# A dynamic convolution and a gated feed-forward on one core: a re-ordered ramp, and x tiles loaded whole

## The chip, the cores and the metric

The kernel runs on one core of a Trainium2 chip. The metric is the device time of one execution in microseconds (us); quoted times are medians of the runs of one kernel. The core has the engines PE (matmul; its weight loads are listed apart as PEld), DVE (VectorE), ACT (ScalarE), POOL (GpSimd) and SP (SyncE, which here only issues DMA), and 16 DMA engines.

A profile is of one execution. Its span is some 1.9 us shorter than the time of the same execution (before: span 767.6, time 769.51), so spans are compared with spans only.

## The reference, cut to what matters

```python
# x: (8, 4096, 192), weight_gen: (8, 4096, 8 heads, 7 taps)
w = softmax(weight_gen, axis=-1)
x_pad = concatenate([zeros((8, 6, 192)), x], axis=1)       # causal: 6 rows of zeros first
out[b, s, h, g] = sum over k of w[b, s, h, k] * x_pad[b, s + k, h, g]
# then, on all 32,768 tokens
h = out @ w_in             # 192 -> 2048
g = h - tanh(h)
return g @ w_out           # 2048 -> 192
```

## The kernel before

The tokens are taken in 32 blocks of 1,024. A partition holds 8 consecutive tokens and the 6 rows ahead of them (the halo). Four blocks make one sequence of 4,096, so blocks 0, 4, 8, ..., 28 start a sequence, and partition 0 of those needs zeros for a halo.

For a block, POOL scales the softmax weights (wsm) and makes seven tap products of 2.9 us, into the tiles even, odd and last. One accumulating DMA then adds the odd taps to the even ones. PE sums what is left by matmuls with an identity (tile pc); this stretch has small matmuls close together, and I call it the conv stretch. ACT evicts it as convT. (Blocks 0 to 2 go without the accumulating DMA: PE sums all their taps.) PE then does the first matmul into ph, ACT a tanh, DVE the subtraction into gt, and PE the second matmul into an output bank (obank), one block behind.

```python
xpool = ctx.enter_context(tc.tile_pool(name="xpool", bufs=2))
...
def load_x(n):
    ...
    if n == 0:
        rows(0, P, HALO, HALO + J); rows(16, P, 0, HALO); rows(1, 16, 0, HALO)
        no_halo()                      # copies a row of zeros into the halo of partition 0
    elif s == 0:                       # start of a sequence
        no_halo()
        rows(0, 1, HALO, HALO + J)
        rows(1, 16)
        rows(16, P)
    else:
        rows(0, P)                     # the whole tile, 1,344 KB
...
for n in range(NTOT):
    if n + 3 < NTOT:
        load_wg(n + 3)
        load_x(n + 3)
    for p in range(J):
        gemm1(n, 2 * p); gemm1(n, 2 * p + 1)
        ...
        if p == 0 and 1 <= n < NTOT - 2:
            products(n + 2, behind=last_sub[0] if n > 1 else None)
        if 1 <= n < NTOT - 1 and p == 6:
            ...                        # conv stretch of block n + 1
```

xpool has two buffers, so the load of block n + 2 is issued when POOL ends its last tap of block n: POOL's pace sets the moment of every x load. And the argument `behind` holds POOL's scale until PE and DVE have come far enough, so that POOL can't run away from them.

The softmax here doesn't subtract the row's maximum and nothing guards it: scores larger than these inputs give would overflow.

## Time and profile before

| | before |
|---|---|
| time, median of 3 runs | 768.26 us (768.07 to 768.48) |
| the profiled run | 769.51 us, span 767.6 us |
| POOL, one block | 22.64 us, without a pause in it |
| PE, one block, undisturbed | 22.56 us |
| chain of what ended last | PE 93% |

The prediction below shows the views that it rests on. Beside them, the page gives these: first the busy time of each engine (share of the span, number of instructions), then two groups of instructions (line, engine, operation, tiles, shapes and count; busy time and mean ns of one; idle time before them and what ended it).

```profile
PE 737.2 (96%) x14784; PEld 577.8 (75%) x14784; DVE 652.8 (85%) x595; ACT 637.1 (83%) x865; POOL 695.3 (91%) x290
...
L197 POOL TENSOR_TENSOR odd<-x_t,wsm 128x1536 bf16<-128x1536 f32 x93 | 270.0, 2904 | 0.0
...
L206 POOL DMA_DIRECT2D even<-odd x29 | 34.9, 1205 | 9.1 <-POOL odd L197 9.1
```

POOL's 91% hides that it is full: its work ends near 713 us, and 695.3 us of it are done by then. So PE and POOL are bound together, and what matters is how far PE runs behind POOL. I measure that as a **distance**: from POOL's issue of the accumulating DMA of a block to PE's first conv matmul of that block. A large distance means that PE has fallen behind. It can't be much under 8.8 us, since the DMA itself lands 8.8 us (median) after its issue.

PE's waits after the ramp (40 to 760 us; what PE waited for, us in total, times, longest) are short. Most of their time is "issue", that is, a wait for nothing that the profile names; these are its two longest lines:

```profile
PE pc L240 <- issue: 4.5, 6, 3.2
PE obank L306 <- issue: 0.6, 1, 0.6
```

PE's instructions come in pages by DMA (queue q8 of the profile, "instruction", moved 1.88 MB in 115 packets, 16 KB each).

### The profile page before, as it was taken

The numbers are of one execution on the slowest core, as the hardware profiler recorded it, in microseconds if no ns is written. First come the engines' busy times: TensorE is split into PE (matmuls) and PEld (weight loads), VectorE is DVE, ScalarE is ACT, GpSimd is POOL, SyncE is SP. The second block draws the span as 40 slices with busy tenths as digits, with TensorE's granted clock in tenths as the row PEclk, the third lists the DMA queues.
The fourth block names the chain that finished last, engine by engine and source line by source line (L and its number), as shares of the span: only waits on it lengthen the run. The fifth ranks groups of instructions, "written<-read, shape, count | busy, mean of one in ns | idle before, by whom it ended". The sixth has DMA issues, their size and how long they took to land.

```text
span 767.6 us, 32329 instructions
## 1 busy us (share of the span) xinstructions
PE 737.2 (96%) x14784; PEld 577.8 (75%) x14784; DVE 652.8 (85%) x595; ACT 637.1 (83%) x865; POOL 695.3 (91%) x290
## 2 busy tenths in 40 slices
PE   2798999999999999999999999999999999999997
PEld 2276787777777777777777777777778777777777
DVE  7886898888888888889888889888888988888883
ACT  1876888888888888888888888888888888888883
POOL 6999999999999999999999999999999999999100
PEclk9999999999999999999999999999999999999999
DMA  7913776555677555577655567755556765542412
GB/s 216 202 56 87 182 181 161 119 138 150 164 182 176 135 129 145 149 178 183 166 125 129 150 160 182 180 126 139 144 149 175 182 174 114 129 141 77 98 44 84
DMA packets 25989, 111.37 MB, mean 145 GB/s; under 512 B 4815, under 2 KB 9855, under 8 KB 21893
## 3 DMA queue, kind: packets, MB, share of 16 engines
q1 hardware_dynamic: 14830, 77.00, 30.2%
q0 software_dynamic: 10816, 31.99, 25.8%
q8 instruction: 115, 1.88, 1.0%
q10 hardware_dynamic: 208, 0.34, 0.2%
q14 instruction: 20, 0.16, 0.1%
HBM read 54.49 MB, written 25.17 MB: 104 GB/s over the span
## 4 chain that ended last, share of the span: by engine, by line
PE 93%; DVE 3%; POOL 1%; issue 1%; DMA 1%; ACT 0%; SPq 0%; POOLq 0%
PE obank L306 43%; PE ph L273 43%; PE pc L240 6%; DVE gt L285 2%; PE po L341 1%; DMA x_t<-zero 1%; POOL even L197 1%; ACT th L284 0%; POOL odd L197 0%; SPq L107 0%; DVE zr L156 0%; DVE zsum L150 0%; ACT convT L254 0%; SPq L93 0%; DVE out_sb L353 0%
## 5 line engine op out<-in xcount | busy, mean ns | idle before, releaser
L285 DVE TENSOR_TENSOR gt<-ph,th 128x1024 bf16<-128x1024 f32 x512 | 602.7, 1220 | 94.6 <-ACT th L284 92.1
L284 ACT ACTIVATE th<-ph 128x1024 f32<-128x1024 f32 x512 | 497.4, 1022 | 65.9 <-PE ph L273 65.2
L306 PE MATMUL obank<-w_out,gt 64*128 64x192 bf16 x7936 | 399.2, 243 | 1.4 <-issue 0.6
L306 PEld LDWEIGHTS <-gt 64*128 64x128 bf16 x7936 | 351.4, 94 | 52.6 <-issue 1.2
L273 PE MATMUL ph<-convT,w_in 64*128 64x512 bf16 x3072 | 384.8, 378 | 6.3 <-DVE gt L285 5.1
L197 POOL TENSOR_TENSOR even<-x_t,wsm 128x1536 bf16<-128x1536 f32 x94 | 273.0, 2904 | 3.1 <-DMA x_t<-zero 0.7
L197 POOL TENSOR_TENSOR odd<-x_t,wsm 128x1536 bf16<-128x1536 f32 x93 | 270.0, 2904 | 0.0
L273 PEld LDWEIGHTS <-w_in 64*128 64x128 bf16 x3072 | 176.4, 94 | 112.1 <-issue 18.8
L325 ACT ACTIVATE out_sb<-obank 128x192 f32<-128x192 f32 x248 | 82.4, 332 | 30.6 <-PE obank L306 23.5
L197 POOL TENSOR_TENSOR last<-x_t,wsm 128x1536 bf16<-128x1536 f32 x31 | 103.4, 3335 | 0.0
L240 PE MATMUL pc<-ident,even 64*128 64x64 bf16 x2304 | 70.3, 191 | 3.7 <-POOL even L197 2.4
L240 PEld LDWEIGHTS <-even 64*128 64x128 bf16 x2304 | 64.7, 96 | 5.0 <-POOL even L197 2.7
L254 ACT ACTIVATE convT<-pc 128x1024 bf16<-128x1024 f32 x64 | 48.8, 808 | 14.9 <-PE pc L240 14.8
L206 POOL DMA_DIRECT2D even<-odd x29 | 34.9, 1205 | 9.1 <-POOL odd L197 9.1
L168 POOL TENSOR_TENSOR wsm<-e_t,zr 128x448 f32<-128x448 f32 x30 | 41.7, 1391 | 0.0
L240 PE MATMUL pc<-ident,last 64*128 64x64 bf16 x768 | 23.2, 192 | 8.5 <-DVE last L197 8.3
L140 ACT ACTIVATE e_t<-wg_t 128x448 f32<-128x448 f32 x32 | 18.5, 577 | 7.0 <-DMA wg_t<-in_weight_gen_dram 7.0
L240 PEld LDWEIGHTS <-last 64*128 64x128 bf16 x768 | 17.0, 96 | 8.7 <-DVE last L197 8.3
L240 PE MATMUL pc<-ident,odd 64*128 64x64 bf16 x448 | 16.2, 199 | 6.7 <-issue 3.9
L150 DVE TENSOR_REDUCE zsum<-e_t 128x64 f32<-128x448 f32 x32 | 19.5, 609 | 3.0 <-ACT e_t L140 3.0
L156 DVE RECIPROCAL zr<-zsum 128x64 f32<-128x64 f32 x30 | 16.6, 554 | 3.0
L240 PEld LDWEIGHTS <-odd 64*128 64x128 bf16 x448 | 11.8, 100 | 7.4 <-issue 4.2
(20 smaller groups left out, 48.7 us busy)
## 6 DMA issues: line engine op xcount, KB each, us to landing
x_t<-in_x_dram SPq DMA_DIRECT2D x24, 1344.0 KB
even<-odd POOLq DMA_DIRECT2D x29, 1024.0 KB, 8.8
out_dram<-out_sb SPq DMA_DIRECT2D x31, 768.0 KB
x_t<-in_x_dram SPq DMA_DIRECT2D x7, 1176.0 KB
wg_t<-in_weight_gen_dram SPq DMA_DIRECT2D x32, 224.0 KB
x_t<-in_x_dram SPq DMA_DIRECT2D x7, 157.5 KB
x_t<-in_x_dram SPq DMA_DIRECT2D x1, 768.0 KB
w_out<-in_moe_w_out_dram POOLq DMA_DIRECT2D x1, 768.0 KB, 9.1
```

What stands on the lines that cost most here:

```text
L140: nc.scalar.activation(out=e_t[:].rearrange("p j h k -> p (j h k)"), in_=wg_t[:].rearrange("p j h k -> p (j h k)"), func=ACT.Exp,)
L150: nc.vector.reduce_sum(out=zsum[:], in_=e_t[:].rearrange("p j h k -> p (j h) k"), axis=AX.X)
L168: return eng.tensor_mul(wsm.rearrange("p j h k -> p (j h) k"), e_t[:].rearrange("p j h k -> p (j h) k"), zr.rearrange("p (n o) -> p n o", ...
L197: eng.tensor_mul(dst[k].rearrange("p c j h g -> p j h c g"), x_t[:, k : k + J, :].rearrange("p j (h c g) -> p j h c g", h=H, c=NC), w[:, : ...
L206: nc.gpsimd.dma_start(out=even[:].rearrange("p i c j h g -> p (i c j h g)")[:, 0:ACC], in_=odd[:].rearrange("p i c j h g -> p (i c j h g)" ...
L240: nc.tensor.matmul(pc[:, r, col : col + R], lhsT=prods[c][gi][r * R : (r + 1) * R, c, 2 * j : 2 * j + 2].rearrange("p j h g -> p (j h g)") ...
L254: nc.scalar.activation(out=conv_of[n][:, c0 : c0 + nch, :].rearrange("p c (j r t) -> p r (c j) t", r=2, t=R), in_=pc[:, :, 0 : nch * JH * ...
L273: nc.tensor.matmul(ph[:, r, :], lhsT=w_in[r * R : (r + 1) * R, c, f * P : (f + 1) * P], rhs=convT[r * R : (r + 1) * R, c, :], start=(c == ...
L284: last_act[0] = nc.scalar.activation(out=th[:], in_=ph_f, func=ACT.Tanh)
L285: last_sub[0] = nc.vector.tensor_sub(gt[:], ph_f, th[:])
L306: mm = nc.tensor.matmul(po[:, 0:D], lhsT=g_of[n][f][r * R : (r + 1) * R, col : col + P], rhs=w_out[r * R : (r + 1) * R, f, :], start=(r == ...
L325: last_act[0] = nc.scalar.activation(out=out_sb[:, j, :], in_=po[:, 0:D], func=ACT.Copy)
```

## The change

The intent: let POOL start its first tap before the halo has come, let PE begin block 1 earlier, and simplify the x loads at the starts of sequences. In words: the taps of block 0 are split by tokens, so that pieces that need no halo run first, between DVE and POOL; the loads of w_in start with the first exponential; ACT copies the first seven tiles of w_in to the upper partitions where a DMA did; x of block 1 waits for a product of block 0; the conv sums of block 1 are made in the idle output banks; block 1's weights are scaled on POOL; and every x tile but the first is one load, with the zero copy after it.

```diff
-        elif s == 0:
-            no_halo()
-            rows(0, 1, HALO, HALO + J)
-            rows(1, 16)
-            rows(16, P)
         else:
-            rows(0, P)
+            dma = rows(0, P)
+            if behind is not None:
+                order(dma, behind, "order of the loads")
+            if s == 0:
+
+                no_halo()
...
+    load_w_in(0, FA, last_exp[0])
     softmax_norm(0, obank[0])
...
     products(
         0,
-        on_vector=(6, 3, 4, 5),
-        order_of=(6, 0, 3, 1, 4, 5, 2),
-        sums=(6, 3, 0, 4, 5, 1, 2),
-        hooks={2: rest_of_w_in},
+        taps=[
+            (G_, 6, 0, J),     # engine, tap, first and last token of a partition
+            (V, 5, 1, J),
+            (V, 4, 2, J),
+            (V, 5, 0, 1),
+            (V, 4, 0, 2),
+            (G_, 0, 0, J),
+            (V, 3, 0, J),
+            (V, 2, 0, J),
+            (G_, 1, 0, J),
+        ],
+        sums=(6, 5, 4, 3, 0, 2, 1),
+        hooks={1: rest_of_w_in},
     )
+    load_x(1, first_halo[0])
...
+    for c in range(NC):
+        nc.scalar.activation(out=w_in[R:P, c, 0:FA], in_=w_in[0:R, c, 0:FA], func=ACT.Copy)
...
+                if p == 3:
+                    pcs = []
+                    sums = conv_sums(1, ((0, 1),), pcs, obank)
```

(The comment on the tuple is mine; the moves of the softmax of blocks 2 and 3 and some helpers are cut.)

More of the change, by code (lines that the diff above doesn't have):

```diff
@@ L78 @@
     last_sub = {}
-    last_wsm = {}
+    last_exp = {}
+    first_halo = {}
     def order(inst, other, reason):
@@ L97, in load_wg, with load_x @@
         wg_of[n] = wg_t
-    def load_x(n):
+    def load_x(n, behind=None):
         b, s = divmod(n, NSB)
@@ L105, in rows @@
         def rows(p0, p1, r0=0, r1=HALO + J):
-            win = x[b, s0 + p0 * J - HALO + r0 : s0 + p0 * J - HALO + r0 + 1]
-            nc.sync.dma_start(
+            first = x[0, 0:1]
+            return nc.sync.dma_start(
                 out=x_t[p0:p1, r0:r1, :],
                 in_=bass.AP(
-                    tensor=win.tensor,
-                    offset=win.offset,
+                    tensor=first.tensor,
+                    offset=first.offset + (b * S + s0 + p0 * J - HALO + r0) * D,
                     ap=[[J * D, p1 - p0], [D, r1 - r0], [1, D]],
@@ L139, in softmax_exp @@
         e_t = wgpool.tile([P, J, H, K], FP32, name="e_t")
-        nc.scalar.activation(
+        last_exp[0] = nc.scalar.activation(
             out=e_t[:].rearrange("p j h k -> p (j h k)"),
@@ L152, in softmax_norm @@
         )
+        zr = wgpool.tile([P, J * H], FP32, name="zr")
         wsm = wgpool.tile([P, J, H, K], FP32, name="wsm")
         if bank is None:
-            zr = wgpool.tile([P, J * H], FP32, name="zr")
             nc.vector.reciprocal(zr[:], zsum[:])
@@ L158, in softmax_norm @@
             return
-        zr = bank[:, 512 - J * H : 512]
-        nc.vector.reciprocal(zr, zsum[:])
+        zr_v = bank[:, 512 - J * H : 512]
         wsm_v = bank[:, 0 : J * H * K].rearrange("p (j h k) -> p j h k", j=J, h=H)
-        scale(nc.vector, wsm_v, e_t, zr)
-        last_wsm[0] = scale(nc.vector, wsm[:], e_t, zr)
-        wsm_of[n] = (wsm, wsm_v, None, None)
+        nc.vector.reciprocal(zr_v, zsum[:])
+        if n == 0:
+            scale(nc.vector, wsm[:], e_t, zr_v)
+        else:
+            nc.vector.tensor_copy(zr[:], zr_v)
+        scale(nc.vector, wsm_v, e_t, zr_v)
+        wsm_of[n] = (wsm, wsm_v, None if n == 0 else e_t, zr)
     def scale(eng, wsm, e_t, zr):
@@ L172, in scale, with products @@
         )
-    def products(n, on_vector=(), order_of=None, sums=None, hooks={}, behind=None):
+    def products(n, taps=None, sums=None, hooks={}, behind=None):
         x_t = x_of.pop(n)
@@ L194, in products @@
             hooks[-1]()
-        for k in order_of or range(K):
-            eng, w = (nc.vector, wsm_v) if k in on_vector else (nc.gpsimd, wsm[:])
-            eng.tensor_mul(
-                dst[k].rearrange("p c j h g -> p j h c g"),
-                x_t[:, k : k + J, :].rearrange("p j (h c g) -> p j h c g", h=H, c=NC),
-                w[:, :, :, k : k + 1]
+        for eng, k, j0, j1 in taps or [(nc.gpsimd, k, 0, J) for k in range(K)]:
+            w = wsm_v if eng is nc.vector else wsm[:]
+            mul = eng.tensor_mul(
+                dst[k][:, :, j0:j1].rearrange("p c j h g -> p j h c g"),
+                x_t[:, k + j0 : k + j1, :].rearrange("p j (h c g) -> p j h c g", h=H, c=NC),
+                w[:, j0:j1, :, k : k + 1]
                 .rearrange("p j h (k o) -> p j h k o", o=1)
-                .to_broadcast([P, J, H, NC, GC]),
+                .to_broadcast([P, j1 - j0, H, NC, GC]),
             )
+            if j1 == 1:
+                first_halo[0] = mul
             if k == K - 2 and in_pairs:
@@ L220, in products, with conv_sums @@
             prods_of[n] = [[dst[k] for k in (sums or range(K))]] * NC
-    def conv_sums(n, parts, pcs):
+    def conv_sums(n, parts, pcs, home=None):
         prods = prods_of[n]
@@ L227, in conv_sums @@
             conv_of[n] = cpool.tile([P, NC, HT], BF16, name="convT")
-        pcs.extend(psum_h.tile([P, 2, HT], FP32, name="pc", tag="ph") for _ in parts)
+        for _ in parts:
+            pcs.append(home or psum_h.tile([P, 2, HT], FP32, name="pc", tag="ph"))
         if parts[-1][-1] == NC - 1:
@@ L240, in conv_sums @@
                             nc.tensor.matmul(
-                                pc[:, r, col : col + R],
+                                pc[r][:, col : col + R] if home else pc[:, r, col : col + R],
                                 lhsT=prods[c][gi][
@@ L253, in conv_out @@
             c0, nch = chunks[0], len(chunks)
-            nc.scalar.activation(
-                out=conv_of[n][:, c0 : c0 + nch, :].rearrange(
-                    "p c (j r t) -> p r (c j) t", r=2, t=R
-                ),
-                in_=pc[:, :, 0 : nch * JH * R].rearrange("p r (cj t) -> p r cj t", t=R),
-                func=ACT.Copy,
-            )
+            out = conv_of[n][:, c0 : c0 + nch, :].rearrange("p c (j r t) -> p r (c j) t", r=2, t=R)
+            cols = nch * JH * R
+            if isinstance(pc, list):
+                for r in range(2):
+                    nc.scalar.activation(
+                        out=out[:, r],
+                        in_=pc[r][:, 0:cols].rearrange("p (cj t) -> p cj t", t=R),
+                        func=ACT.Copy,
+                    )
+            else:
+                nc.scalar.activation(
+                    out=out,
+                    in_=pc[:, :, 0:cols].rearrange("p r (cj t) -> p r cj t", t=R),
+                    func=ACT.Copy,
+                )
     def conv(n, *parts):
@@ L370 @@
     FA = 7 * P
-    def load_w_in(f0, f1):
-        for c in range(NC):
-            src = moe_w_in[c * GC : c * GC + 1, f0:f1]
-            dma = nc.gpsimd.dma_start(
-                out=w_in[0:R, c, f0:f1],
-                in_=bass.AP(
-                    tensor=src.tensor,
-                    offset=src.offset,
-                    ap=[[G * F, H], [F, GC], [1, f1 - f0]],
-                ),
-            )
-            if f0 == 0:
-                order(dma, last_wsm[0], "order of the loads")
@@ L388, in copy_w_in, with w_in_rows, load_w_in @@
-    def copy_w_in(f0, f1, eng):
-        eng.dma_start(out=w_in[R:P, :, f0:f1], in_=w_in[0:R, :, f0:f1])
+    def w_in_rows(c, f0, f1):
+        src = moe_w_in[c * GC : c * GC + 1, f0:f1]
+        return bass.AP(
+            tensor=src.tensor, offset=src.offset, ap=[[G * F, H], [F, GC], [1, f1 - f0]]
+        )
+    def load_w_in(f0, f1, behind=None):
+        for c in range(NC):
+            dma = nc.gpsimd.dma_start(out=w_in[0:R, c, f0:f1], in_=w_in_rows(c, f0, f1))
+            if c == 0 and behind is not None:
+                order(dma, behind, "order of the loads")
@@ L391, in rest_of_w_in @@
     def rest_of_w_in():
         load_w_in(FA, F)
+    V, G_ = nc.vector, nc.gpsimd
     load_wg(0)
     load_x(0)
+    load_wg(1)
     softmax_exp(0)
+    load_w_in(0, FA, last_exp[0])
     softmax_norm(0, obank[0])
-    load_wg(1)
-    load_x(1)
-    load_w_in(0, FA)
     products(
         0,
-        on_vector=(6, 3, 4, 5),
-        order_of=(6, 0, 3, 1, 4, 5, 2),
-        sums=(6, 3, 0, 4, 5, 1, 2),
-        hooks={2: rest_of_w_in},
-    )
+        taps=[
[11 more added lines that the diff above has]
+        hooks={1: rest_of_w_in},
+    )
@@ L408 @@
+    load_x(1, first_halo[0])
+    load_wg(2)
     softmax_exp(1)
+    for c in range(NC):
+        nc.scalar.activation(out=w_in[R:P, c, 0:FA], in_=w_in[0:R, c, 0:FA], func=ACT.Copy)
     softmax_norm(1, obank[1])
-    load_wg(2)
-    copy_w_in(0, FA, nc.scalar)
-    copy_w_in(FA, F, nc.sync)
-    products(1, on_vector=(0, 1), hooks={4: load_w_out})
+    nc.sync.dma_start(out=w_in[R:P, :, FA:F], in_=w_in[0:R, :, FA:F])
+    products(
+        1,
+        taps=[(V, 0, 0, J), (V, 1, 0, J)] + [(G_, k, 0, J) for k in range(2, K)],
+        hooks={4: load_w_out},
+    )
@@ L414, with some @@
     conv(0, (0, 1), (2,))
+    softmax_exp(2)
     load_x(2)
+    softmax_norm(2)
+    products(2)
+    def some(sums, m):
+        for _ in range(m):
+            next(sums, None)
     for n in range(NTOT):
@@ L422 @@
             gemm1(n, 2 * p + 1)
-            if n == 0 and p == 1:
-                softmax_exp(2)
+            if n == 0:
+                if p == 3:
+                    pcs = []
+                    sums = conv_sums(1, ((0, 1),), pcs, obank)
+                if 3 <= p <= 6:
+                    some(sums, (3 if p == 3 else 1) * 4 * JH)
+                if p == 7:
+                    some(sums, K * 4 * JH)
+                    conv_out(1, ((0, 1),), pcs)
+                    conv(1, (2,))
+                continue
             if p == 5 and n + 3 < NTOT:
                 softmax_exp(n + 3)
-            if n >= 1 and (p < 6 or n == NTOT - 1):
+            if p < 6 or n == NTOT - 1:
                 gemm2((n - 1) * J + p)
-            if p == 0 and 1 <= n < NTOT - 2:
-                products(n + 2, behind=last_sub[0] if n > 1 else None)
-            if n == 0 and p == 7:
-                conv(1, (0, 1))
-                conv(1, (2,))
+            if p == 0 and n == 1:
+                softmax_exp(3)
+            if p == 1 and n == 1:
+                softmax_norm(3)
+                products(3)
+            if p == 0 and 1 < n < NTOT - 2:
+                products(n + 2, behind=last_sub[0])
             if 1 <= n < NTOT - 1 and p == 6:
@@ L447 @@
                 gemm2((n - 1) * J + 7, 0, FILL)
-            if n == 0 and p == 2:
-                softmax_norm(2)
-                products(2)
             if p == 6 and n + 3 < NTOT:
```

## The prediction

> **What bounds the kernel now.** The time is 768.26 us. I read first the chain of what ended last: PE holds 93%, POOL 1%, which says matmuls are everything. So I then asked whether the busiest helper has any slack, and read the groups of instructions and the timeline of POOL over one later block of 1,024 tokens.
>
> ```profile
> PE 93%; DVE 3%; POOL 1%; issue 1%; DMA 1%; ACT 0%; SPq 0%; POOLq 0%
> ...
> 599.59 1.41 POOL L168 TENSOR_TENSOR wsm<-e_t,zr 128x448 f32<-128x448 f32 x1
> ...
> 618.59 1.20 POOL L206 DMA_DIRECT2D even<-odd  x1 [0.30 <-POOL odd L197]
> ...
> 622.23 1.42 POOL L168 TENSOR_TENSOR wsm<-e_t,zr 128x448 f32<-128x448 f32 x1
> ```
>
> POOL's block is 622.23 - 599.59 = 22.64 us and it never waits inside it. PE's block, from one convT eviction to the next in that region, is 22.56 us when nothing disturbs it, and 22.70 on average over blocks 3 to 31. So two engines are bound at once, and POOL runs uninterrupted from 9.53 us to its end near 713 us.
>
> The change is all in the ramp, so the third view is the chain of waits over the first 80 us (start, length, what).
>
> ```profile
> 2.66 6.70 DMA x_t<-zero
> 9.53 2.90 POOL even L197
> 12.43 1.66 POOL odd L197
> 15.26 2.91 POOL even L197
> 18.86 1.03 ACT convT L254
> 23.77 5.75 DVE gt L285 x5
> 30.64 9.04 DVE gt L285 x8
> 64.29 3.17 issue
> ```
>
> Read it so: the halo of x of block 0 lands at 9.36; three POOL taps of 2.87 follow; block 0 of the first matmul is then paced by DVE (16 subtractions at about 1.14 and two softmax pairs at about 1.17), until the first matmul of block 1 at 43.05. At 64.29 PE stands still for 3.17 us, waiting for nothing that the profile names. The windows view shows what follows (stretch, PE, weight loads, DVE, ACT, POOL, granted clock, DMA share, GB/s).
>
> ```profile
> 66.00:68.00 2.00, 0.54 (x22) 0.54 (x23) 0.00 (x0) 0.00 (x0) 2.00 (x2) 0.88 0.00 0
> 68.00:70.00 2.00, 2.00 (x28) 1.18 (x24) 0.00 (x0) 0.60 (x1) 2.00 (x2) 0.50 0.04 8
> 70.00:72.00 2.00, 2.00 (x33) 1.34 (x29) 0.90 (x1) 1.82 (x2) 2.00 (x2) 0.77 0.00 0
> ```
>
> Half clock from about 67.5 to 70.9, 3.4 us, costs some 1.7 us more: convT to convT is 27.65 us there against 22.56.
>
> **What stands still at 64.29.** The queue table has the answer:
>
> ```profile
> q8 instruction: 115, 1.88, 1.0%
> ```
>
> 1.88 MB in 115 packets is 16 KB each; 29,568 loads and matmuls of PE over 115 is 257 instructions per packet. In the trace's DMA records the packet for this stop starts at 65.07, though PE began the page before it at 62.0, and PE goes on at 67.46, 2.4 us after the packet starts. The x load of block 4 was issued at 58.13 and landed at 65.64: the fetch sat behind it. Over all later fetches I took the delay from the start of a page to the fetch of the next: 3.3 to 4.9 us for nearly all asked for in the first 7 us after an x load was issued, about 1.1 us at 9 to 15 us after it, near 0 beyond. A page lasts 7.7 us in the matmul stretches and only 3.1 to 5 us in the dense conv stretch, so only the conv stretch can run dry.
>
> [...] DVE and POOL taps overlap in this trace at 1.75 and 2.90, the usual lengths, so I charge nothing.
>
> **The change, part by part.**
>
> *Start of POOL.* The three w_in issues (1.93 us) wait for the exponential, which ends at 3.99, not for the weights at 6.56: with the 0.3 us of delay seen before, 4.3 to 6.25. Their packets came 4 us after issue in this trace (6.88 to 10.9), so they now come at about 8.3, when the halo's bytes have mostly gone (last packet ends 8.27): the halo still lands at 9.0 to 9.4. Tap 6, which needs no halo, starts at about 6.35 and ends at 9.25; tap 0 at 9.5, tap 1 to 15.2, against 18.1 before. One tap is gained: 2.9 us.
>
> *POOL afterwards.* Issues of the rest of w_in 1.7 us, then, new, the scaling of block 1 on POOL, 0.97 us (its length at 35.35). Tap 2 of block 1 starts at 17.9 instead of 19.80. x of block 1, held until DVE's first halo piece at 9.8, needs 6.3 to 7 us as later tiles did, and lands at 16 to 17, just in time. **POOL gains 2.9 - 0.97 = 1.9 us**, kept for the whole run since POOL never waits.
>
> *PE to the end of block 0.* conv of 0 ends 2.9 us earlier, but DVE is now in front: x of 1 at 16.0, two taps 3.35, softmax pair of 2 1.17, so the first subtraction is at about 20.6 (22.49 before). Sixteen at 1.145 end at 39.0; the conv of 1 now goes through the output banks in idle PE time and only its last third, about 0.5 us, is left: block 1 begins at 39.5, 3.5 us earlier. The ScalarE copies of w_in, three of about 0.9 us (estimate: 0.577 us at 448 columns and 1.02 at 1,024), end by 15 beside this. Softmax of 3 in block 1 fits in the 0.90 us DVE idles before 50.94; some 0.2 lost. PE leads by 3.3.
>
> *The stop.* x of block 4 is now one whole load behind POOL's 54.5 (before: zero, three pieces, main piece 1.7 us after POOL). It ends near 61; the fetch goes then and PE resumes at about 63.2, against 67.46. PE would run dry at 64.1 - 3.3 = 60.8, a stop of 2.4 us[...]. PE is then 4.3 + 85% of 1.6 = **5.6 us** ahead.
>
> *What remains.* PE is now 5.6 ahead but POOL, and with it every x load, only 1.9. From the issue of the accumulating DMA to the first conv matmul it was 14.7 us at block 3 and 15.7 at the last block; now it starts at 14.7 - 3.7 = 11.0. The DMA lands after 8.0 to 10.8, so products are there. But the x load is issued 4.2 us after that DMA, so conv pages are now asked for in the middle of it. By hand: block 3's conv page (3.7 us) was asked for 10.9 us after the load; now at about 7.2, delay 3.2 + 2.3 to arrive = 5.5, stop 1.8. Block 4's (4.5 us without its stop) was at 7.5; now at 5.6, delay 3.8 + 2.3 = 6.1, stop 1.6. The distance is back at about 14.2 after two blocks, where the kernel before also began; from there both drift to about 15.6. **So PE's extra 3.7 us is given back but for some 0.4 us.** Gain: 1.9 + 0.4 = 2.3, time 766.0; I put the middle at 765.8, since the seven shorter x loads may save one stop.
>
> **Rivals.** (A) The lead is kept: conv pages happen to fall well, and the gain is PE's 5.6, bounded by POOL at 1.9 + 4.9 (slack of the last block: conv at 725.27, DMA landed at 720.35), 762 to 763. For it: the chain names PE almost alone, and pages move 9/16 per block, so some convs are split over two slow pages. Against: in the kernel before, distances under 15.5 cost 0.35 to 0.8 us every second block. 20%. (B) The ramp gains less: halo or x of 1 late by 1 us costs POOL about as much; 767. For it: w_in now shares the engines with the halo; against: the 4 us delay of its packets. 20%. (C) Taps or copies collide so that the ramp loses: 769. Little speaks for it; 4%.
>
> **Range and chances.** Main line 765 to 766.5; A pulls down, B up: 763.0 to 767.3. Two per cent is 15.4 us, more than the whole stop and ramp lead together, so faster 0.01, slower 0.01.
>
> **What would show it.** Right: POOL's first tap at about 6.4 and tap 2 of block 1 at 17.9; first matmul of block 1 near 39.5; the stop in block 1 shorter and no half clock; later stops of 1 to 2 us in blocks 3 and 4 under "issue"; POOL still 22.65 per block without waits, its last tap some 1.9 us earlier. Wrong: PE's lead over POOL at the end larger by 2 us or more (then A), POOL waiting for x of 1 or the halo (then B), or POOL's block changed.

Its sum: the gain was 1.9 (POOL) + 0.4 (PE) = 2.3 us, that is 768.26 - 2.3 = 766.0, with the middle put at 765.8. The 85% in PE's lead (4.3 + 85% of 1.6 = 5.6) is my own guess at the chance that the clock stays full in block 1, and no run here showed its ground; the 1.6 is about what half clock cost in the trace of the kernel before. There PE stood still from 64.29 to 67.46, and the clock records show half clock from 67.50 to 70.91.

## The result, and the profile after

| | before, same rounds | after | ratio (95% interval) |
|---|---|---|---|
| first | 768.37 us (4 runs) | 767.96 us (767.65 to 769.62, 4 runs) | 0.9995 (0.9976 to 1.0015) |
| repeated later | 768.83 us (9 runs) | 768.24 us (767.94 to 770.16, 5 runs) | 0.9997 (0.9983 to 1.0011) |

A ratio is the mean time of one kernel's fast runs over that of the other's of the same rounds, so it is not quite the ratio of the medians that I quote. An execution over 1.5% above the fastest of its kernel counts as slow and is left out of the ratios. The time is the same; it lies above the predicted range of 763.0 to 767.3.

The ramp did what it was made for. POOL's timeline of the changed kernel (start, length, engine, line, operation):

```profile
6.30 2.94 POOL L202 TENSOR_TENSOR last<-x_t,wsm 128x1536 bf16<-128x1536 f32 x1
...
16.57 1.00 POOL L172 TENSOR_TENSOR wsm<-e_t,zr 128x448 f32<-128x448 f32 x1
17.65 2.90 POOL L202 TENSOR_TENSOR even<-x_t,wsm 128x1536 bf16<-128x1536 f32 x1
```

Tap 2 of block 1, the last line, starts at 17.65, against 19.80 before: POOL is 2.2 us ahead. The chain of waits of the first 95 us (start, length, what):

```profile
9.65 5.96 DMA x_t<-in_x_dram
...
23.91 13.69 DVE gt L301 x12
...
38.30 1.53 PE ph L289 x12
...
59.55 2.34 issue
61.89 0.59 PE pc L248 x29
...
87.06 2.70 issue
89.77 0.91 PE obank L322 x17
```

The first matmul of block 1 starts at 38.30, against 43.05. The stop of block 1 is 2.34 us long instead of 3.17. PE resumes at 61.89 and not at 67.46, so it is 5.6 us ahead there, and 7.1 us at the conv of block 3 (82.66 against 89.72). Then comes the new stop at 87.06. The windows view shows what it brings (stretch, PE, weight loads, DVE, ACT, POOL, granted clock, DMA share, GB/s):

```profile
88.00:90.00 2.00, 0.23 (x6) 0.24 (x8) 1.39 (x2) 0.00 (x0) 2.00 (x2) 1.00 0.08 24
90.00:92.00 2.00, 2.00 (x27) 1.59 (x23) 0.00 (x0) 0.71 (x2) 2.00 (x1) 0.73 0.04 8
92.00:94.00 2.00, 2.00 (x24) 1.68 (x21) 0.87 (x1) 1.67 (x2) 2.00 (x2) 0.50 0.00 0
```

PE is idle for nearly all of 88 to 90, and from 90.93 to 94.35 the granted clock is 0.50. The kernel before paid this price once, at 67.5; the changed one avoids it there and pays it at 90.9. This is so in the first profile only: in the repeat the same stop (2.67 us, to 89.75) brought no half clock, and the distance at block 4 below is 12.4 there and not 14.2.

PE's waits after the ramp, in the same form as those of before:

```profile
PE pc L248 <- issue: 5.3, 5, 2.3
PE obank L322 <- issue: 4.6, 4, 2.7
```

They are longer in sum, not shorter. Counted in both traces with PE's 32 semaphore instructions, every 256th instruction of PE begins a page: there are 115 such places, as many as packets, and all stops of over 0.5 us between 40 and 760 us (two before, seven after) end at one. The time after 40 us in which neither a matmul nor a weight load ran just before such a place sums to 5.4 us before and 10.0 us after, so nearly all of the "issue" stands at page boundaries. The distances tell where the lead went:

| distance, us | block 3 | 4 | 5 | 10 | 11 | 14 | 15 | 31 |
|---|---|---|---|---|---|---|---|---|
| before | 14.7 | 14.6 | 14.9 | 15.5 | 15.4 | 15.4 | 15.9 | 15.7 |
| after | 9.8 | 14.2 | 14.8 | 15.6 | 16.7 | 16.4 | 18.0 | 17.2 |
| after, repeated | 9.7 | 12.4 | 14.1 | 15.6 | 16.4 | 16.2 | 18.1 | 15.8 |

By block 5 PE has given back nearly all that it had gained on POOL. From then on it falls further behind than before, in two steps, at blocks 11 and 15, in both profiles. The second step is a stop of 1.5 us by the chain of waits (1.9 in the repeat), at 340.84. The DMA issues of SP just ahead of it (start, length, line), in the changed kernel:

```profile
326.18 0.34 SPq L108 DMA_DIRECT2D x_t<-in_x_dram  x1
335.15 0.73 SPq L118 DMA_DIRECT2D x_t<-zero  x1
335.94 0.42 SPq L345 DMA_DIRECT2D out_dram<-out_sb  x1
336.48 0.36 SPq L94 DMA_DIRECT2D wg_t<-in_weight_gen_dram  x1
```

and in the kernel before:

```profile
328.35 0.72 SPq L117 DMA_DIRECT2D x_t<-zero  x1
329.12 2.43 SPq L107 DMA_DIRECT2D x_t<-in_x_dram  x3
331.66 1.66 SPq L329 DMA_DIRECT2D out_dram<-out_sb  x1
333.36 1.72 SPq L93 DMA_DIRECT2D wg_t<-in_weight_gen_dram  x1
```

This is the load of block 16, which starts a sequence. The zero copy writes where the whole load has just written, so it must wait until that has landed, 9 us after its issue. SP's issues stand in the listing in the program's order, so the output store (768 KB) and the load of weight_gen (224 KB) stand behind the zero copy. They now go out from 335.94 on, not just behind the x load, and the conv stretch starts at 338.45: the store's issue is 2.5 us ahead of it, where it was 7.9 us ahead before. The page begun at 338.0 has its successor fetched only at 340.2, when the store has landed (339.9), and PE stands until 342.35.

After the second step POOL too has to wait for DVE and so for PE (the "pace" dependency), at 349.36 (and for 0.2 us at 508.09). From the view of POOL's waits between 300 and 350 us:

```profile
POOL wsm L172 <- DVE gt L301: 0.6, 1, 0.6
```

The repeat has the same wait (0.7 us at 349.49), the kernel before has none. Between these waits POOL's period from block to block stays at 22.65 us. It had kept 2.17 us of gain at block 3 (accumulating DMA at 72.82 against 74.99); at the last block 1.33 us are left (708.21 against 709.54), 1.46 in the repeat.

### The profile page after: what moved, and what is told of

Read it like the earlier page. It is cut to its first block, busy times and chain, and to the rows that moved or that the text cites. A ratio compares the mean times of both kernels' runs of the same rounds, so it can differ in the third digit from the quotient of the medians.

```text
span 767.7 us, 32312 instructions
## 1 busy us (share of the span) xinstructions
PE 737.8 (96%) x14784; PEld 581.2 (76%) x14784; DVE 652.2 (85%) x597; ACT 640.0 (83%) x869; POOL 696.5 (91%) x291
## 3 DMA queue, kind: packets, MB, share of 16 engines
q1 hardware_dynamic: 14718, 77.03, 28.8%
## 4 chain that ended last, share of the span: by engine, by line
PE 93%; DVE 3%; issue 2%; DMA 1%; ACT 1%; DVEq 0%
PE obank L322 43%; PE ph L289 43%; PE pc L248 6%; DVE gt L301 2%; PE po L357 1%; DMA x_t<-in_x_dram 1%; DVE odd L202 0%; DMA wg_t<-in_weight_gen_dram 0%; DVE even L202 0%; ACT th L300 0%; DVE zsum L151 0%; DVE obank L172 0%; ACT convT L266 0%; ACT e_t L141 0%; DVE obank L163 0%
## 5 line engine op out<-in xcount | busy, mean ns | idle before, releaser
L202 POOL TENSOR_TENSOR even<-x_t,wsm 128x1536 bf16<-128x1536 f32 x93 | 270.1, 2904 | 2.4
L289 PEld LDWEIGHTS <-w_in 64*128 64x128 bf16 x3072 | 178.9, 94 | 108.3 <-issue 18.2
L202 POOL TENSOR_TENSOR last<-x_t,wsm 128x1536 bf16<-128x1536 f32 x32 | 106.4, 3324 | 0.0
L272 ACT ACTIVATE convT<-pc 128x512 bf16<-128x512 f32 (+1 forms) x63 | 47.9, 805 | 7.9 <-PE pc L248 7.9
L172 POOL TENSOR_TENSOR wsm<-e_t,zr 128x448 f32<-128x448 f32 x31 | 38.5, 1241 | 0.7 <-DVE gt L301 0.7
L248 PEld LDWEIGHTS <-last 64*128 64x128 bf16 x768 | 17.3, 96 | 10.2 <-POOL last L202 9.3
L248 PE MATMUL pc<-ident,odd 64*128 64x64 bf16 x400 | 14.8, 199 | 5.7 <-issue 4.5
```

Source lines behind the costliest of these rows:

```text
L172: return eng.tensor_mul(wsm.rearrange("p j h k -> p (j h) k"), e_t[:].rearrange("p j h k -> p (j h) k"), zr.rearrange("p (n o) -> p n o", ...
L202: mul = eng.tensor_mul(dst[k][:, :, j0:j1].rearrange("p c j h g -> p j h c g"), x_t[:, k + j0 : k + j1, :].rearrange("p j (h c g) -> p j h ...
L248: nc.tensor.matmul(pc[r][:, col : col + R] if home else pc[:, r, col : col + R], lhsT=prods[c][gi][r * R : (r + 1) * R, c, 2 * j : 2 * j + ...
L272: nc.scalar.activation(out=out, in_=pc[:, :, 0:cols].rearrange("p r (cj t) -> p r cj t", t=R), func=ACT.Copy,)
L289: nc.tensor.matmul(ph[:, r, :], lhsT=w_in[r * R : (r + 1) * R, c, f * P : (f + 1) * P], rhs=convT[r * R : (r + 1) * R, c, :], start=(c == ...
```

## The experiments

My theory had two parts. **First**, PE's lead is given back in the early conv stretches, because their pages are asked for in the middle of an x load, whose moment POOL sets. **Second**, the whole loads at sequence starts cost late stops, because of the zero copy's place on SP's queue. The rivals were: the second loss is only where page boundaries happen to fall; the ramp gains less than it seems; and whole loads are harmless, with the loss coming from something else that the change moved.

### The old loads at sequence starts, in the new kernel

```diff
+        elif s == 0:
+            no_halo()
+            rows(0, 1, HALO, HALO + J)
+            rows(1, 16)
+            rows(16, P)
         else:
             dma = rows(0, P)
             ...
-            if s == 0:
-                no_halo()
```

> The changed kernel with the x loads of sequence starts as they were before: zero rows first, then row group 0, 1 to 15, 16 to 127. Theory H (the zero copy behind the whole load makes the sync queue wait, so that the output store and the next weight load run into the conv stretch): the two stops of 1.28 us at 252.65 and 1.70 us at 342.35 shrink under 0.7 us, the distance from the accumulating DMA to the conv at the end falls from 17.2 to about 16 us, the time falls by about 1.2 us to 766.7. Theory D (PE's lead is given back whatever the form of these loads, and only the POOL start counts): time within 0.4 us of the changed kernel, 767.7. Rival N (nothing but noise between the two kernels): the same as both, 768.

Measured: 767.65 us (766.85 to 768.01), ratio 0.9984 (0.9971 to 0.9996). The stops at blocks 10 and 14 are gone, and the distance is 15.8 at block 15 and 15.3 at the last, for 18.0 and 17.2. The stops follow the loads' form. The time fell less than I expected: 1.0 us below the kernel before of its rounds, where the changed kernel is 0.4 to 0.6 below. Its profiled run was the shortest of its five. The intervals of the two ratios overlap, so the stops are shown to go with the loads' form, but a gain in time over the changed kernel is not shown by this run.

### The whole loads alone, in the kernel before

```diff
-        elif s == 0:
-            no_halo()
-            rows(0, 1, HALO, HALO + J)
-            rows(1, 16)
-            rows(16, P)
         else:
             rows(0, P)
+            if s == 0:
+                no_halo()
```

> The kernel before with only the whole-tile x loads at sequence starts, zero copy behind them. Theory H: about 1 us slower than before, 769.2, with stops over 1 us in blocks whose load is that of a sequence start (POOL's pace is untouched, the distance at the end rises from 15.7 to about 17). The stop of 3.36 us at 67.46 may shrink, since the load of block 4 starts 1.6 us earlier, but that is given back. Theory that whole-tile loads help: 766 to 767.5, with the gain from that first stop kept to the end.

(The run also takes over the changed kernel's way of computing the address of a load.)

Measured: 769.82 us (769.5 to 770.93) beside 768.69 of before, ratio 1.0017 (1.0004 to 1.003). So this part alone makes the old kernel slower. In its profile the distance goes from 15.9 to 17.3 in one step at block 27, after a stop at 617.90 in a block whose x load starts a sequence; it ends at 16.7. The first stop, of block 1, shrank from 3.17 to 1.18 us, and that was given back (distance 11.5 at block 3, 14.7 at block 6). POOL was also 0.5 us later from its ramp on (75.49 against 74.99 at block 3), in code that the edit doesn't touch: its first tap started at 10.03 and not at 9.53, since the halo of block 0 landed later. So not all of the 1.1 us need come from the loads.

### The zero copy behind the store

The load stays whole, and only the zero copy is issued later: behind the output store and the load of weight_gen.

```diff
             if s == 0:
-
-                no_halo()
+                late_halo.append(no_halo)
...
         if n + 3 < NTOT:
             load_wg(n + 3)
+            if late_halo:
+                late_halo.pop()()
             load_x(n + 3)
```

> The changed kernel, whole-tile loads kept, but the zero copy issued behind the output store and the weight load of the next block, so that the sync queue never waits for an x load before the store. Theory H: the stores go out 1.5 us after the x load also at sequence starts, stops of 1.28 and 1.70 us vanish or fall under 0.7 us, time about 766.5, as in the run with the old loads or 0.2 us better. Theory D: 767.7.

Measured: 766.83 us (766.74 to 767.17), ratio 0.9977 (0.9963 to 0.9991). SP's issues for the same block:

```profile
326.15 0.33 SPq L109 DMA_DIRECT2D x_t<-in_x_dram  x1
326.54 1.36 SPq L345 DMA_DIRECT2D out_dram<-out_sb  x1
327.95 0.97 SPq L95 DMA_DIRECT2D wg_t<-in_weight_gen_dram  x1
336.44 0.73 SPq L119 DMA_DIRECT2D x_t<-zero  x1
```

The store goes 9.4 us earlier and has landed by 338.3, and there is no stop in that conv stretch: its identity matmuls run through without an "issue" in the chain. The distance is 15.7 at block 15 and 15.0 at the end. The load is as whole as in the changed kernel; only its companion's place differs. This edit was run again beside the changed kernel, to be sure of the size.

> The changed kernel itself, unedited, in the same rounds as the next three. 767.9 us (767.4 to 768.4), against before 768.5; its stops at sequence-start loads (over 1 us around 252 and 342 us) again in the trace.

> The zero copy behind the store and the weight load once more, beside the changed kernel: theory H expects it 0.8 to 1.4 us below the changed kernel of the same rounds, 766.8; if the first difference was drift between chips, the two are within 0.3 us.

Measured in the same rounds: 768.24 us for the changed kernel (ratio to before 0.9997), and 766.41 us for the late zero copy (766.05 to 767.6; ratio 0.9968, 0.9956 to 0.9981). The intervals don't touch. The difference of the medians is 1.8 us, and so is that of the profiled spans (766.2 and 764.4). In the two profiles, POOL's last accumulating DMA is 1.0 us earlier (707.07 against 708.08) and the last distance 0.7 shorter (15.1 against 15.8), which makes 1.7. These are the two terms that the theory names, but for 0.24 us by which POOL was ahead at block 3 already (72.70 against 72.94).

### The x loads held out of the conv stretch

Here the first part is tested. Each x load of the loop waits for the last conv matmul before it.

```diff
-                            nc.tensor.matmul(
+                            last_conv[0] = nc.tensor.matmul(
...
             load_wg(n + 3)
-            load_x(n + 3)
+            if n == 0:
+                load_x(n + 3)
...
                 conv(n + 1, (2,))
+                if n + 3 < NTOT:
+                    load_x(n + 3, last_conv[0])
```

> The changed kernel with each x load from block 4 on held until the last conv matmul of the block before has run (the load is then issued after the dense conv stretch instead of 11 to 13 us before it). Theory F (instruction fetches of PE stand behind the x loads, and these stops give PE's lead back): the stops at conv vanish but for some 0.3 us where an accumulating DMA runs; PE keeps the 7 us that it led by at block 3, the distance from accumulating DMA to conv stays at 9.5 to 11 us, time 761 to 762.5, bound by POOL at 22.65 us a block. If the stops come from something else (dense issue itself, weight loads), they stay, and the time is 767 to 768. If the load then comes too late for POOL, POOL waits for x and the time is above 768.

Measured: 761.22 us (761.09 to 761.67), ratio 0.9903 (0.989 to 0.9917). PE's waits after the ramp:

```profile
PE pc L249 <- DMA even<-odd: 2.0, 4, 0.6
...
PE pc L249 <- issue: 0.6, 1, 0.6
```

The load of block 5, for one, now goes out behind the start of the conv stretch of block 3 (80.90), where the changed kernel issued it at 77.03, ahead of the stretch (82.66):

```profile
83.40 0.33 SPq L109 DMA_DIRECT2D x_t<-in_x_dram  x1
```

The sum of "issue" is 0.6 us, where it was 9.9. PE now waits for the accumulating DMA, which means that it has caught up with POOL: the distance is 8 to 10 us to the end. POOL has come into the chain on the page, where PE held 93% before:

```profile
POOL 51%; PE 40%; DMA 5%; issue 2%; DVE 1%; ACT 0%; POOLq 0%
```

How much of the chain each holds depends on four waits of some 0.5 us, since the two engines' blocks differ by under 0.1 us: in the repeat below it is PE 66%, POOL 28%. The distance is the surer sign. The lead is kept as soon as no large x load stands in the conv stretch. A second run beside the last ones gave the same time:

> The held x loads once more, as the base for the next run: 761.2 us.

Measured: 761.24 us (760.44 to 763.01), ratio 0.9902 (0.9887 to 0.9916). Its profile kept one stop of 1.1 us, to 60.27, and a sum of "issue" of 1.4 us.

### The same hold, in the kernel before

```diff
+            if s == 0:
+                no_halo()
+                parts = [rows(0, 1, HALO, HALO + J), rows(1, 16), rows(16, P)]
+            else:
+                parts = [rows(0, P)]
+            if behind is not None:
+                for dma in parts:
+                    order(dma, behind, "order of the loads")
```

and the loop as above.

> The kernel before (old ramp, old load forms) with the x loads from block 4 on held until the conv of the block before has run. If PE's lead is lost only to instruction fetches behind x loads, the old ramp also runs up to the accumulating DMA's landing and is then bound by POOL, which starts 2.2 us later than in the changed ramp: 763.4 us (762.8 to 764), the distance from accumulating DMA to conv falling from 15.7 to about 10. The difference to the held loads under the changed ramp (761.22) is then what the ramp is worth: 2.2 us. If the old ramp stays at 768, the holding only works together with the changed ramp.

Measured: 762.96 us (762.43 to 763.29), ratio 0.9928 (0.9916 to 0.994). So most of the gain of the hold has nothing to do with the ramp. With the loads held in both, the ramp is worth 762.96 - 761.22 = 1.7 us (2.0 us when each is taken from the kernel before of its own rounds), and POOL's lead at block 3 is 74.51 - 72.73 = 1.8 us. The old ramp's POOL varies from profile to profile with the landing of the first halo (first tap at 9.08 here, 9.53 in the kernel before, 10.03 with the whole loads), so this lead is known to some 0.5 us. That is POOL's share of the ramp, as the prediction had it (1.9). The ramp gains what it should; what was lost was lost after it.

### The pages shifted

64 matmuls that nobody reads (128 instructions, half a page) are put at the start.

```diff
+    shift = psum_h.tile([P, 2, HT], FP32, name="shift", tag="ph")
+    for i in range(64):
+        nc.tensor.matmul(
+            shift[:, 0, 0:R], lhsT=ident[0:R, :], rhs=ident[0:R, 0:R], start=True, stop=True
+        )
```

> The changed kernel with 64 extra weight loads and 64 extra matmuls of the identity, never read, ahead of everything on PE, where it idles: 128 instructions, half a page, so that each page of instructions begins 128 instructions earlier in the program. Theory F (fetches of pages): the stop of 2.5 us at 61.89 vanishes (under 0.6 us), because the page boundary now falls in the middle of that conv and the page before it is asked for ahead of the load; the stops of later blocks move to other blocks and places; the time stays within 1 us of the changed kernel, since what PE gains is given back: 767 to 768.2. If the stops are tied to the conv itself or to data, they stay where they are.

Measured: 767.38 us (767.15 to 768.05), ratio 0.9989 (0.9976 to 1.0002). Between 40 and 80 us PE has no "issue" wait any more. This is all that it waited for there:

```profile
PE obank L322 <- ACT th L300: 0.4, 1, 0.4
```

The stop of 2.3 us is gone, though no DMA was changed. Others came instead: 1.10 us to 85.15, 2.62 to 112.61, 1.02 to 203.73, 0.88 to 433.78. The distance starts at 8.9, and is back at 15.1 by block 9 and at 15.3 at the end. So where a page boundary falls decides which conv stretch stops. The idle time at page boundaries is 7.2 us in sum, for 10.0, and the time is not clearly apart from that of the changed kernel. Shifting pages is no cure.

This profile also bears on the second part. The load of block 16 and the store behind it go out as late as in the changed kernel (326.48 and 335.68), yet PE runs without a pause from 338 to 344, and POOL has no pace wait. So a late store alone doesn't stop PE. The page that begins there at 339.03 was fetched at 333.78, ahead of the store; the one that stopped the changed kernel was asked for at 338.0, behind it. The rival that the second loss depends on where page boundaries fall is thus half right.

### An idle load put back into the conv stretch

In the kernel with the held loads, a load of the same rows into a tile that nobody reads is issued where the old x load was.

```diff
             if n == 0:
                 load_x(n + 3)
+            else:
+                idle_load(n + 3, last_tap[n + 1])
```

> The changed kernel with held x loads, plus a load of the same rows into a tile that nothing reads, issued where the x load was before (when POOL has done its last tap). It puts the transfer back into the conv stretch without any consumer. Theory F: the fetches are late again, stops of 0.5 to 3 us at the conv come back in most blocks until the distance is 15 us or more, time 766 to 769 (also because the engines carry 1.3 MB more per block). If it was not the transfer but the wait on the x buffer or the order on the sync queue that held PE, the time stays at 761 to 762.

Measured: 778.21 us (775.86 to 787.71, 6 runs), ratio 1.0129 (1.0107 to 1.015). The run of 787.71 counts as slow; the five fast ones lie at 775.86 to 782.3, with a median of 777.52. PE's waits and then POOL's, of this kernel's profile:

```profile
PE pc L265 <- issue: 10.8, 10, 2.5
```

```profile
POOL even L218 <- DMA x_t<-zero: 5.8, 2, 3.2
POOL even L218 <- PE ph L306: 5.0, 2, 3.7
```

The stops are back, ten of them in the conv line alone, though the x loads themselves are still held and nobody waits for the idle ones. It is a load's presence in that stretch that stops PE, not a dependency of PE on it. The time is worse than I expected, because a second effect came in that I had not planned. POOL waits four times, 10.8 us in sum, each time in a block that starts a sequence (12, 20, 24 and 28). The view names PE for two of these waits, but by the semaphores of the trace the last thing to come in all four was the zero copy. It is issued when the held x load has landed (255.66 for block 12), the idle load goes out just behind it (258.11), and it lands only at 262.51; POOL goes on at 262.67. So this run shows the mechanism; its 778 us is no measure of its size.

### Scaling block 1 on DVE, in the kernel with held loads

```diff
-        if n == 0:
-            scale(nc.vector, wsm[:], e_t, zr_v)
-        else:
-            nc.vector.tensor_copy(zr[:], zr_v)
+        scale(nc.vector, wsm[:], e_t, zr_v)
```

> The changed kernel with held x loads, and the weights of block 1 scaled by DVE again (as in the kernel before) in place of 0.97 us on POOL. With held loads POOL is the bound (PE waits for the accumulating DMA), so POOL starting 0.9 us earlier should shorten the run by 0.7 to 1.0 us: 760.3 us. If PE's lead from the ramp is the limit instead, DVE's extra 0.6 us costs as much: 761.2 to 761.8.

Measured: 760.63 us (759.56 to 761.27), ratio 0.9897 (0.9884 to 0.9909), which overlaps with the run without it. In its profile x of block 1 landed at 17.55, and POOL, which no longer had the scale to do, waited 1.05 us for it. This run is inconclusive by itself. It shows that the scale on POOL had been free as long as x of block 1 is the last to come.

### The same, with x of block 1 released earlier

x of block 1 is released by DVE's first piece instead of its first halo piece.

```diff
-            if j1 == 1:
+            if j0 == 1:
                 first_halo[0] = mul
```

> Held x loads, block 1 scaled by DVE, and x of block 1 released by DVE's first piece (ends near 8.1 us) in place of the halo piece (near 9.6). In the earlier run with DVE's scaling POOL waited 1.05 us for a late engine of that load (landed 17.55). If that wait was what ate the 0.97 us, POOL's first tap of block 1 now starts near 16.7 in place of 17.7 and the run is 0.7 to 1 us below the held loads: 760.3 us. If the load only slows w_in and the halo, no gain: 761 to 762.

Measured: 760.01 us (759.93 to 760.54), ratio 0.9884 (0.9871 to 0.9898), beside 761.24 for the held loads alone and 768.83 for the kernel before. x of block 1 is issued at 8.07 and has landed at 15.37. POOL's first product of block 1 starts at 16.70, against 17.65 after the change:

```profile
16.70 2.93 POOL L200 TENSOR_TENSOR even<-x_t,wsm 128x1536 bf16<-128x1536 f32 x1
```

Most of this gain of 0.95 us is still there at the last block (706.27 against 707.10 in the run with held loads alone), and the time is 1.2 us shorter. This is the fastest version: 8.8 us, or 1.2%, below the kernel before.

## Why the prediction was right and wrong

**What bounds the kernel: right.** PE and POOL within 0.1 us per block, and the fetch behind the x load as the cause of the stops. The held loads confirm it: without x loads in the conv stretch, "issue" shrinks to 0.6 us (1.4 in the repeat), and PE waits for POOL's accumulating DMA instead. The prediction's reading of the fetch delays holds on redoing, if a little rounded: pages asked for in the first 7 us after an x load waited 2.3 to 5.0 us in all but one case. It left out that the delay rises again, up to 4.6 us, for pages begun 21 us or more after a load, just ahead of the next one. In the six longest stops of the changed kernel the fetch started 1.4 to 6.1 us after the page before it had begun, and PE went on 2.2 to 2.6 us after the fetch had started.

**The start of POOL: right.** First tap at 6.30 (6.35 predicted), tap 2 of block 1 at 17.65 (17.9), gain 2.17 us (1.9), and no wait for the halo or for x of block 1. Rival B's signs did not appear.

**PE to the end of block 0: right, slightly small.** Block 1 began at 38.30 (39.5), so PE was 4.75 us ahead for 3.5.

**The stop in block 1: right, with some luck.** 2.34 us (2.4), the clock stays full, PE 5.6 us ahead (5.6). That the clock would stay full was my own guess, and these runs don't show what decides it: with the old loads a stop of 2.07 us there was followed by half clock (at 62.26), and of the two stops at block 3 the one of 2.70 us was (at 90.93), its repeat of 2.67 us was not.

**The give-back: right in kind, and sharper.** Distance at block 3 of 9.8 (11.0), and a stop there of 2.70 us (1.8), which in one of two profiles brought half clock; the prediction had not foreseen that. By block 5 the distance was 14.8, and the lead was gone, as predicted. Rival A failed as the kernel stood; the held loads show that it would have come true with another moment of the loads (761.2).

**The step that failed is the last term of the sum:** "from there both drift to about 15.6", with the middle lowered because "the seven shorter x loads may save one stop". I counted on the loads being shorter and did not read what the zero copy, now behind its load, does to the order of SP's issues. It moves the store's issue close to the conv stretch ahead of a sequence start (2.5 us ahead of it at block 14, for 7.9), and a page that is asked for behind it there comes late. This cost two stops (1.04 us to 252.65 and 1.51 to 342.35), took the distance to 18, and let PE pace POOL, which so lost 0.7 us of its gain in waits. The term has the wrong sign. Where I put a small gain, the measurement is a loss of 1.8 us (766.41 against 768.24 in the same rounds). With the zero copy behind the store, the kernel ran 1.9 and 2.4 us under the kernel before of its rounds, which is about the 2.3 us that the rest of the sum had predicted.

**One smaller fault of method.** I took the drift to the end from one profile and the time from three other runs. The profiled run of before took 769.51 us, 1.25 above the median that I subtracted from, so its end distance was likely above that of a usual run. From its own time the main line of the sum would have given 769.51 - 2.3 = 767.2. The same holds for the first profile of the changed kernel (769.62, against a median of 767.96); its repeat fell at the median, and there the last distance is 15.8 instead of 17.2.

**What stays open.** Restoring the old loads took the late stops away but gained less than the late zero copy (767.65 against 766.83 in the same rounds). Which of its four issues costs that, I have not separated; the intervals of the two ratios overlap. Nor did I run the late zero copy with shifted pages, so how much of its 1.8 us hangs on where the boundaries fall stays open. The 0.5 us by which POOL was later in the old ramp with whole loads is no riddle: the first halo landed later in that profile, and earlier in another one with the same ramp.

## What to carry to other kernels

When two engines are bound together, follow the distance between them from block to block: a lead of one that the other does not share can be given back when something else, here the fetch of instructions behind a large load, ties them (the distance went from 9.8 us at block 3 to 14.8 at block 5). On SP's queue a zero copy that waited 9 us for the x load held back the store and the load behind it (335.94 and 336.48, against 326.54 and 327.95 with the zero copy last), so a change to a load must be read together with the order of all issues of that engine. And a large load can be moved out of the stretch that consumes instructions fastest (a page lasts 3.1 to 5 us in the conv stretch here, 7.7 in the matmul stretches): this was worth 5.5 us in the old kernel (768.45 to 762.96) and 7.0 us in the new one (768.24 to 761.24), far more than the ramp.
